# Turning q in 64x64 tiles, nine tokens a partition, next to the scores of the preceding pair

## The chip, the cores and the metric

The kernel runs on one core of one Trainium2 chip. The metric is device time in microseconds, the median of several executions. Shorter is better.

A core has five engines that run at the same time and meet at semaphores. TensorE (PE) multiplies matrices and turns (transposes) tiles, and writes to PSUM. VectorE (DVE) and ScalarE (ACT) read PSUM and compute on elements. GpSimd (POOL) computes on elements in SBUF. SyncE (SP) issues most of the DMA transfers here. Each engine takes its instructions strictly in the order in which the program gives them, and an instruction that waits holds up those behind it on its engine. For SP that makes a queue: a transfer can't be issued before the ones ahead of it have been.

## The reference

Eight batches of eight heads with 576 tokens of 64 numbers go through an attention of two parts, and the sum goes through a layer with an ELU between two matrix products. Cut to its core:

```python
q_d, k_d, v_d = means of 4 neighbouring tokens           # 144 coarse tokens
out_up = repeat(softmax(q_d k_d^T / 8) v_d, 4)           # far part
mask = abs(pos[:, None] - pos[None, :]) < 4
out_local = softmax(where(mask, q k^T / 8, -1e9)) v      # near part
x = (out_up + out_local) as [4608 tokens, 8 heads * 64 = 512]
h = x @ w_in                                             # 512 -> 2048
out = where(h > 0, h, exp(min(h, 0)) - 1) @ w_out        # 2048 -> 512
```

All arrays come in and go out as float32. On PE the kernel computes in float16.

## The kernel before

**Pairs.** Two heads are handled together and make a pair; a batch has four (j = 0 to 3). Heads e = 0 and 1 of a pair stand on partitions 0 to 63 and 64 to 127, with the 64 numbers of a head along the partitions and the tokens along the free dimension. To get q into this form it must be turned. For batches 2 to 7 this goes in five steps:

1. `load_qk` (line 206) loads q and k of a pair as float32 through SP. q comes as 96 partitions with six tokens of each of the two heads, k from batch 3 on as 96 partitions with twelve rows of 64.
2. `cast_qk` (line 232) has POOL cast both to float16. q's cast also brings the two heads of a token next to each other (line 242). Behind each cast a copy of one element (`apart`, line 230) marks its end.
3. `transposes` (line 314) turns q on PE: six transposes of 96 partitions x 128 columns (line 329) into the PSUM tile `tqk`. For batches 0 and 1, cast by the DMA, the heads are turned one by one into the upper and the lower half (line 324). k is turned on PE up to batch 2; from batch 3 on `flip` (line 804) does it by a transposing DMA, issued on SP as soon as POOL has cast k.
4. `evict_q` (line 355) has ACT copy q to SBUF in the order of the tokens (line 359).
5. `sums` (line 374) forms the coarse tokens: for q on POOL in two adds (lines 395, 397), for k on DVE (line 378).

`pair_transposes` (line 813) calls steps 3 to 5.

**Scores and outputs.** `pair_scores` (line 901) computes the near scores, 20 matmuls on 64x64 tiles (line 459), and the coarse ones (line 472, 8 matmuls), ACT takes the exponential (line 482) and DVE multiplies by the mask (line 497). `denominators` sums for a whole batch (line 519), DVE takes the reciprocal `rc` (line 525). For batches 3 to 7 the reciprocals are spread over the partitions by way of DRAM: `spread_out` (line 531) writes `rc` to `rd`, and `spread_in` (line 540) reads it back, repeated, as `rcb`, in two transfers. Both are issued on SP. `pair_outputs` multiplies by v (lines 603, 623), in batches 3 to 6 for pairs 0 and 1 together and then for pairs 2 and 3; `normalise` has DVE multiply by `rcb` (lines 667, 672) and POOL add the near and the far part into `xt` (line 684).

**The layer.** The 4608 tokens are cut into nine blocks of 512. `mm1` (line 720, four matmuls a step, 16 steps a block) and `mm2` (line 740, four matmuls a step) are interleaved, mm2 one block behind. Between them ACT takes the exponential (line 724) and DVE finishes the ELU (lines 725, 726). The attention of the next batches runs in between these steps.

**PSUM.** The tiles `tqk`, `sc`, `vs` and `lg` of two banks come from one turn of buffers (`two`, line 134), two of them once the first stage is over. A tile can be written when the earlier tile in its buffer has been read.

**The order** is written out by hand. Each action is an event with a time, and the program is issued in the order of these times; they aren't microseconds but slots, one step of mm1 and one of mm2 each, 16 to a block. For batches 4 to 7 the times stand in `LATER` (4 to 6) and `LAST` (7), counted from the first step of mm1 of the block with the batch's number; `tr` is `pair_transposes`, `sc` `pair_scores`, `cast` the casts, `dn` the denominators, `so` `spread_out`, `si` `spread_in`, `out` `pair_outputs`. Since a block is 16 slots long, the time t of batch b stands at t + 16 in the count of batch b - 1. Around a cast stand, from line 983 on:

```python
            at(p["cast"][j], cast_v, b, j)
            if b > 1:
                at(p["cast"][j] - 0.1, cast_qk, b, j)
                at(p["cast"][j] + 0.1, load, n + 3)
            if b >= FLIP:
                at(p["cast"][j] + 0.02, flip, b, j)
            at(p["tr"][j], pair_transposes, b, j)
            at(p["sc"][j], pair_scores, b, j)
```

`load` (line 968) issues q, k and v (four transfers) of the pair three further on, whose buffers the cast has just read. So the place of a cast also sets where one transposing DMA and six loads stand in SP's queue. The stores of the results (line 748) stand in the same queue.

Of the kernel before, what the change touches and what calls it, by code (L numbers as in the profile page):

```python
# [16 lines left out]
SD = S // 4  # L17
# [21 lines left out]
def _np_consts():  # L39

    f16 = np.float16
    off = np.arange(KW) - PAD
    m = np.zeros((KW, NB, QB), dtype=f16)
    for c in range(NB):
        for u in range(QB):
            ok = (np.abs(off - u) < 4) & (off + QB * c >= 0) & (off + QB * c < S)
            m[ok, c, u] = 1.0
    m = m.reshape(KW, S)
    neg = ((m - 1) * 30000).astype(f16)
    rs = np.zeros((QB, 3, SD), dtype=f16)  # L50
# [10 lines left out]
    return np.eye(KW, dtype=f16), neg, rs.reshape(QB, 3 * SD), vr, ind  # L61


def _np_windows():
# [39 lines left out]
def kernel(  # L104
# [101 lines left out]
    def load_qk(b, j, held=False):  # L206

        got = []
        for src, name in ((q, "q"), (k, "k")):
            a = src[b, 2 * j]  # L210
            t = sb.tile([QB, 2 * NB, D], FP32, tag=name + "32", bufs=3, name=name + "32")
            if held:
                nc.vector.memset(t[0:1, 0, 0:1], 0.0)
            runs_ = name == "q" or b < FLIP
            nc.sync.dma_start(
                out=t[:].rearrange("p (e r) d -> p e (r d)", e=2) if runs_ else t[:],
                in_=bass.AP(
                    tensor=a.tensor, offset=a.offset,
                    ap=[[TPP * D, QB], [S * D, 2], [1, TPP * D]] if runs_
                    else [[D, QB], [QB * D, 2 * NB], [1, D]],  # L220
                ),
            )
            got.append(t)
        qk32[(b, j)] = got
# [7 lines left out]
    def cast_qk(b, j, half=False):  # L232

        got = []
        for t, name in list(zip(qk32.pop((b, j)), ("q16", "k16")))[:: 1 if b < FLIP else -1]:
            x = sb.tile([QB, NB, 2, D], FP16, tag=name, bufs=4, name=name)
            src = t[:].rearrange("p (e c) d -> p c e d", e=2)
            if half:
                act(out=x[:, :, 0, :], in_=src[:, :, 0, :])
                dve(out=x[:, :, 1, :], in_=src[:, :, 1, :])  # L240
            else:
                nc.gpsimd.tensor_copy(out=x[:], in_=src)  # L242
                apart(x[0:1, 0, 0, 0:1])
            got.append(x)
# [69 lines left out]
    def transposes(b, j, fill=(0, 0)):  # L314
# [3 lines left out]
        for x, t, name, n in zip(xs, tr_tiles(b), ("tq", "tk"), fill):  # L318
            s[name] = t
            keep(t, n)  # L320
            for c in range(NB):
                if is_cast(b, j):
                    for e in range(2):
# [31 lines left out]
    def evict_q(b, j, copy):  # L355
        s = st[(b, j)]
        qt = s["q"] = QT[j]
        to, got = in_order(s["tq"], qt[:, 0:S])
        copy(out=to, in_=got)  # L359
        s["qt"] = [qt[:, QB * c : QB * c + QB] for c in range(NB)]  # L360

# [56 lines left out]
    def masked_scores(j, g, sc):  # L418
# [2 lines left out]
        r = [slice(64 * e, 64 * e + 64) for e in range(2)]  # L421
        for e in range(2):
            nc.tensor.matmul(
                sc[0:KW, 512 * e : 512 * e + HB], C["ID"][:],
                C["NEG"][:, HB * g : HB * g + HB], start=True, stop=False,
            )
        for n in range(3):
# [327 lines left out]
    def keep(t, n):  # L755

        for _ in range(n):
            if t.dtype == FP32:
                nc.tensor.matmul(t[:, 0:512], Z[:, 0:128], Z[:, 0:512], start=True, stop=True)  # L759
            else:  # L760
                for _ in range(4):
                    nc.tensor.transpose(t[0:KW, 0:KW], Z[0:KW, 0:KW], C["ID"][:])

    def first():
        nc.vector.memset(Z[:], 0.0)
# [46 lines left out]

    def pair_transposes(b, j):
        transposes(b, j)
        evict_q(b, j, act)
        if b < FLIP:
            evict_k(b, j, act)
# [3 lines left out]
    def selections(name):  # L821

        if name == "SEL":
            t = C[name] = sb.tile([KW, 1280], FP16, tag=name, bufs=1, name=name)
            src, parts = C["ID"], ((0, 5, 0), (5, 5, 64))
            step = 32
        else:
            src = sb.tile([KW, 16], FP16, tag="I4", bufs=1, name="I4")
            nc.vector.tensor_reduce(
                out=src[:], in_=_free(C["ID"][:, 0:1], [[1, 16], [32, NPAIR]]), axis=AX.X, op=AB.add  # L830
            )
            t = C[name] = sb.tile([KW, 1024], FP16, tag=name, bufs=1, name=name)
            parts, step = ((0, 8, 0),), 8
# [64 lines left out]
    def at(time, fn, *args):  # L898
        events.append((time, len(events), fn, args))

    def pair_scores(b, j):
        sc = two("sc")
        scores(j, sc)
        coarse(b, j, sc)
        exps(b, j, sc, 0, WL)
        exps(b, j, sc, WL, SD + SH)
        mask(b, j)
# [67 lines left out]
        2: dict(tr=[8.521, 19.14, 20.81, 24.84], sc=[16.66, 21.68, 23.15, 26.21], cast=[6.002, 15.82, 19.12, 20.36], dn=[28.71], vs=[29.1], sp=[30.02, 30.15, 29.43, 32.38], out=[30.72, 32.86, 33, 33.03], so=[17.79], si=[28.4]),  # L975
        3: dict(tr=[25.32, 29.24, 30.74, 34.58], sc=[28.69, 32, 36.48, 37.89], cast=[21.15, 25.5, 25.89, 28.85], dn=[40.9], vs=[40.84], so=[41.77], si=[43.95], out=[46.72, 47.24, 48.76, 48.78]),
    }
    LATER = dict(tr=[-27.78, -24.81, -17.34, -16.19], sc=[-25.74, -22.03, -14.56, -12.79], cast=[-32.93, -27.69, -22.54, -19.07], dn=[-10.25], vs=[-10.47], so=[-9.791], si=[-6.96], out=[-4.288, -4.511, -3.148, -3.906])
    LAST = dict(tr=[-27.36, -24.54, -17.71, -14.25], sc=[-25.67, -22.06, -15.67, -11.26], cast=[-32.18, -27.83, -24.84, -20.85], dn=[-9.492], vs=[-9.098], so=[-9.367], si=[-5.664], out=[-2.829, -4.665, -4.912, -2.635])
    for b in range(4, B):  # L980
        z = mm1_at(b, 0)
        PLAN[b] = {k: [z + x for x in a] for k, a in (LATER if b < B - 1 else LAST).items()}
    for b in range(1, B):
        p = PLAN[b]
        for j in range(NPAIR):
# [61 lines left out]
```

## Time and profile before

| | before |
|---|---|
| median of 3 runs | 351.66 us (351.36 to 353.28) |
| span of the profiled execution | 355.1 us |
| PE busy | 336.1 us, 95% of the span |
| DVE, ACT, POOL busy | 236.4, 180.3, 160.8 us |
| mean granted clock of PE | 0.976 |
| casts of q on POOL (line 242) | 24, 828 ns each |
| transposes of q on 96 partitions (line 329) | 144 |
| packets of all DMA transfers | 100304, 48.89 MB |

The profiled execution has its span as its only time; it is 1% above the median of the runs that were timed without a profile. In the rows that are shown, L and a number is the line of the kernel, `out<-in` names what is written and read, and x with a number is a count. A row of the timeline gives start and length in microseconds; matmuls overlap, so the time that a group takes is read from its start to the start of the next one. In brackets stands how long the engine was idle before, and what ended that. SPq is SP's queue: its rows are the issuing of a transfer, not the transfer.

### The profile page before, as it was taken

Reading aid. Unit: us, or ns where it says so; the run is one execution under the profiler, and the core shown is the slowest. Engines: PE = TensorE matmul, PEld = TensorE weight load, DVE = VectorE, ACT = ScalarE, POOL = GpSimd, SP = SyncE. Lnnn points to the kernel's source line nnn. Section 1 sums busy time; section 2 is a strip of 40 time slices with the busy share of each in tenths; the row PEclk is TensorE's granted clock in tenths of the full one; section 3 lists DMA queues with packets and bytes.
Section 4 is the critical chain, followed back from the end, with each engine's and each line's share of the span. In section 5 each row is a group of like instructions: output and inputs, shape, how many; then the busy total and the mean of one; then the engine's idle time right before and its main releaser. Section 6 shows DMA issues by size and latency. Waiting matters only on the chain.

```text
span 355.1 us, 10487 instructions
## 1 busy us (share of the span) xinstructions
PE 336.1 (95%) x4288; PEld 185.5 (52%) x4288; DVE 236.4 (67%) x466; ACT 180.3 (51%) x312; POOL 160.8 (45%) x298
## 2 busy tenths in 40 slices
PE   7993998799979999999999999999999999999996
PEld 3762885344545454545454555555455544444443
DVE  2334799566789877987697789768755855555510
ACT  4580587225755664466456645663553444444421
POOL 4464449279495834974397449855300500000000
PEclk9998799959999999999999999999999999999999
DMA  8999979997999698998979796943004010011012
GB/s 173 184 166 203 191 172 216 215 186 185 189 152 224 120 205 168 167 185 174 181 155 206 158 218 144 188 123 61 30 32 118 31 59 30 31 46 43 31 59 89
DMA packets 100304, 48.89 MB, mean 138 GB/s; under 512 B 81617, under 2 KB 95265, under 8 KB 100257
## 3 DMA queue, kind: packets, MB, share of 16 engines
q1 hardware_dynamic: 94417, 41.86, 57.8%
q0 software_dynamic: 5600, 6.26, 10.8%
q8 instruction: 33, 0.54, 0.7%
q10 hardware_dynamic: 240, 0.11, 0.2%
q14 instruction: 14, 0.11, 0.1%
HBM read 41.97 MB, written 9.55 MB: 145 GB/s over the span
## 4 chain that ended last, share of the span: by engine, by line
PE 72%; DMA 13%; DVE 6%; ACT 3%; issue 2%; POOL 2%; SPq 1%; DVEq 0%; POOLq 0%; ACTq 0%
PE op L740 31%; PE hp L720 28%; DMA v<-in_v_dram 6%; DMA rcb<-rd 3%; DMA WO<-in_moe_w_out_dram 3%; DVE ln L672 2%; PE sc L759 2%; PE tqk L329 2%; DMA rd<-rc 2%; PE lg L603 2%; DVE e L725 1%; PE sc L459 1%; ACT e L724 1%; DVE gt L726 1%; PE lg L623 1%
## 5 line engine op out<-in xcount | busy, mean ns | idle before, releaser
L740 PE MATMUL op<-WO,gt 128*128 128x512 f16 (+2 forms) x592 | 147.0, 377 | 1.0 <-DVE gt L726 0.6
L724 ACT ACTIVATE e<-hp 128x512 f16<-128x512 f32 x144 | 86.1, 599 | 110.5 <-PE hp L720 95.7
L720 PE MATMUL hp<-xt,WI 128*128 128x512 f16 x512 | 133.4, 384 | 0.7 <-DVE gt L726 0.5
L726 DVE SCALAR_TENSOR_TENSOR gt<-hp,e 128x512 f16<-128x512 f32 x144 | 99.6, 692 | 6.4
L725 DVE TENSOR_SCALAR e<-e 128x512 f16<-128x512 f16 x144 | 60.7, 421 | 58.1 <-ACT e L724 57.6
L740 PEld LDWEIGHTS <-gt 128*128 128x128 f16 x592 | 55.6, 98 | 62.8 <-issue 3.0
L720 PEld LDWEIGHTS <-WI 128*128 128x128 f16 x512 | 55.5, 115 | 49.6 <-issue 3.1
L684 POOL TENSOR_TENSOR xt<-ln 128x128 f16<-128x128 f16 (+7 forms) x55 | 36.7, 695 | 50.8 <-DVE ln L672 50.8
L482 ACT ACTIVATE pex<-sc 128x580 f16<-128x580 f32 (+1 forms) x56 | 30.2, 596 | 9.7 <-PE sc L472 9.7
L395 POOL TENSOR_TENSOR t<-qt 128x288 f32<-128x288 f16 x27 | 18.1, 671 | 36.8 <-ACT qt L359 36.8
L303 POOL CAST v<-v 128x640 f16<-128x640 f32 (+1 forms) x32 | 24.2, 756 | 21.1 <-DMA v<-in_v_dram 21.0
L746 ACT COPY os<-op 128x512 f32<-128x512 f32 (+2 forms) x37 | 21.4, 577 | 19.3 <-PE op L740 19.1
L378 DVE TENSOR_REDUCE ke<-kt 128x145 f16<-128x580 f16 x28 | 21.0, 751 | 2.4 <-ACT kt L366 2.4
L359 ACT COPY qt<-tqk 128x576 f16<-128x576 f16 x28 | 17.9, 638 | 8.5 <-PE tqk L329 6.7
L699 PE MATMUL hp<-xt,WI 128*128 128x256 f16 x128 | 17.3, 288 | 4.6 <-issue 4.6
L672 DVE TENSOR_TENSOR ln<-lg,rcb 128x580 f16<-128x580 f32 x28 | 21.1, 752 | 0.0
L242 POOL CAST q<-q 96x768 f16<-96x768 f32 x24 | 19.9, 828 | 0.0
L242 POOL CAST k<-k 96x768 f16<-96x768 f32 x24 | 19.8, 825 | 0.1
L699 PEld LDWEIGHTS <-WI 128*128 128x128 f16 x128 | 13.6, 118 | 5.8 <-issue 4.7
L497 DVE TENSOR_TENSOR pex<-pex,MASK 128x580 f16<-128x580 f16 x28 | 14.0, 500 | 3.8 <-ACT pex L482 3.6
L397 POOL TENSOR_TENSOR qd<-t 128x144 f16<-128x144 f32 x27 | 12.4, 461 | 2.1
L459 PEld LDWEIGHTS <-kt 64*64 64x64 f16 x560 | 7.0, 108 | 11.7 <-issue 8.8
(113 smaller groups left out, 271.6 us busy)
## 6 DMA issues: line engine op xcount, KB each, us to landing
out_dram<-os SPq DMA_DIRECT2D x35, 256.0 KB, 2.2
v<-in_v_dram SPq DMA_DIRECT2D x111, 80.0 KB, 4.6
q<-in_q_dram SPq DMA_DIRECT2D x25, 288.0 KB, 4.1
k<-in_k_dram SPq DMA_DIRECT2D x25, 288.0 KB, 5.1
rcb<-rd SPq DMA_DIRECT2D x10, 364.0 KB, 4.6
WI<-in_moe_w_in_dram POOLq DMA_DIRECT2D x4, 512.0 KB, 10.9
WO<-in_moe_w_out_dram POOLq DMA_DIRECT2D x4, 512.0 KB, 9.2
q<-in_q_dram POOLq DMA_DIRECT2D x7, 144.0 KB, 7.2
```

The costliest lines, as they stand in the source:

```text
L242: nc.gpsimd.tensor_copy(out=x[:], in_=src)
L303: nc.gpsimd.tensor_copy(out=v16[:], in_=v32[:].rearrange("p (e c) d -> p c e d", e=2))
L482: nc.scalar.activation(out=s["p"][:, :, a : a + n], in_=g2(sc, a, n), func=AF.Exp, scale=SCALE / 16 if a else SCALE,)
L672: nc.vector.tensor_tensor(out=ln[:, 0 : 2 * WL].rearrange("p (m h u) -> p m h u", h=2, u=WQ), in0=_free(lg[:, 0:1], [[WQ, WM], [512, 2], [ ...
L684: eng.tensor_tensor(out=xt(t)[:, j, t0 - TBLK * t : t1 - TBLK * t], in0=ln[:, a:z], in1=_rep4(ln[:, ga : ga + (z - a) // 4]), op=AB.add,)
L699: nc.tensor.matmul(FS[i][:, 256 * f : 256 * f + 256], w_in(dc, 2 * n + f), xts[0][:, dc, 256 * h : 256 * h + 256], start=(f == dc == 0), s ...
L720: nc.tensor.matmul(hp, w_in(dc, fc), xts[t][:, dc, :], start=(dc == 0), stop=(dc == DMC - 1),)
L724: nc.scalar.activation(out=e, in_=hp, func=AF.Exp)
L725: nc.vector.tensor_scalar(out=e, in0=e, scalar1=1.0, scalar2=-1.0, op0=AB.min, op1=AB.add)
L726: nc.vector.scalar_tensor_tensor(out=to, in0=hp, scalar=0.0, op0=AB.max, in1=e, op1=AB.add)
L740: nc.tensor.matmul(op_[:, a:z], gts[t][:, fc, 128 * tt : 128 * tt + 128], WO[:, fc, a:z], start=(fc == 0), stop=(fc == FCN - 1),)
L746: nc.scalar.copy(out=os_[:, a:z], in_=op_[:, a:z])
```

## The change

q of batches 2 to 7 is loaded in another form. The two heads of a pair have 2 x 576 = 1152 tokens, 128 x 9. Partition p gets the nine tokens from 9p on, 2304 bytes in one run, so head 0 lies on partitions 0 to 63 and head 1 on 64 to 127. The cast on POOL is then 128 partitions x 576 elements in order. q is turned by 18 transposes of 64x64, nine for each head, on the tiles at (0, 0) and (64, 64) in turn; the identity grows from 112 to 128 rows for that. ACT's copy puts the tokens in order with nine instead of six columns apart.

From pair (4, 1) to (7, 3) the turning has no event of its own. It is done in `pair_scores` of the preceding pair: the 18 transposes stand right ahead of the scores, and ACT's copy, POOL's adds and DVE's sum over k between the coarse scores and the exponential. Pairs of batches 2 and 3 and pair (4, 0) keep their events. For batches 4 to 7 some casts get earlier times; `tr` stays in the tables but is no longer used beyond (4, 0).

```diff
@@ load_qk
             a = src[b, 2 * j]
+            if name == "q" and b > 1:
+                t = sb.tile([128, 9, D], FP32, tag="q32", bufs=3, name="q32")
+                if held:
+                    nc.vector.memset(t[0:1, 0, 0:1], 0.0)
+                nc.sync.dma_start(
+                    out=t[:], in_=bass.AP(
+                        tensor=a.tensor, offset=a.offset, ap=[[9 * D, 128], [D, 9], [1, D]]
+                    ),
+                )
+                got.append(t)
+                continue
@@ cast_qk
+            if name == "q16" and b > 1:
+                x = sb.tile([128, 9, D], FP16, tag="q16", bufs=4, name="q16")
+                nc.gpsimd.tensor_copy(out=x[:], in_=t[:])
+                apart(x[0:1, 0, 0:1])
+                got.append(x)
+                continue
@@ transposes
+            if name == "tq" and b > 1:
+                for c in range(9):
+                    for e in range(2):
+                        r = slice(64 * e, 64 * e + 64)
+                        nc.tensor.transpose(t[r, 64 * c : 64 * c + 64], x[r, c, :], C["ID"][r, r])
+                continue
@@ evict_q
+        if b > 1:
+            to = qt[:, 0:S].rearrange("p (a r) -> p a r", r=9)
+            got = _free(s["tq"][:, 0:1], [[1, 64], [64, 9]])
         copy(out=to, in_=got)
@@
     def pair_transposes(b, j):
         transposes(b, j)
+        pair_turned(b, j)
+
+    def pair_turned(b, j):
         evict_q(b, j, act)
@@
+    def joined(b, j):
+
+        n = NPAIR * b + j + 1
+        return divmod(n, NPAIR) if NPAIR * 4 < n < NPAIR * B else None
+
     def pair_scores(b, j):
+        nxt = joined(b, j)
+        if nxt:
+            transposes(*nxt)
         sc = two("sc")
         scores(j, sc)
         coarse(b, j, sc)
+        if nxt:
+            pair_turned(*nxt)
         exps(b, j, sc, 0, WL)
@@
-    LATER = dict(tr=[-27.78, -24.81, -17.34, -16.19], sc=[-25.74, -22.03, -14.56, -12.79], cast=[-32.93, -27.69, -22.54, -19.07], dn=[-10.25], vs=[-10.47], so=[-9.791], si=[-6.96], out=[-4.288, -4.511, -3.148, -3.906])
-    LAST = dict(tr=[-27.36, -24.54, -17.71, -14.25], sc=[-25.67, -22.06, -15.67, -11.26], cast=[-32.18, -27.83, -24.84, -20.85], dn=[-9.492], vs=[-9.098], so=[-9.367], si=[-5.664], out=[-2.829, -4.665, -4.912, -2.635])
+    LATER = dict(tr=[-27.78, -24.81, -17.34, -16.19], sc=[-25.74, -22.03, -14.56, -12.79], cast=[-32.93, -28.69, -25.54, -20.07], dn=[-10.25], vs=[-10.47], so=[-9.791], si=[-6.96], out=[-4.288, -4.511, -3.148, -3.906])
+    LAST = dict(tr=[-27.36, -24.54, -17.71, -14.25], sc=[-25.67, -22.06, -15.67, -11.26], cast=[-32.18, -28.83, -25.84, -20.85], dn=[-9.492], vs=[-9.098], so=[-9.367], si=[-5.664], out=[-2.829, -4.665, -4.912, -2.635])
@@
-            at(p["tr"][j], pair_transposes, b, j)
+            if NPAIR * b + j <= NPAIR * 4:
+                at(p["tr"][j], pair_transposes, b, j)
```

The rest of the diff makes the identity 128x128 and cuts it back to 112 where it was used as such. Batch 3 has its own table, with `so` at 41.77 and `si` at 43.95; block 4 begins at 67.52 in that count.

More of the change, by code (lines that the diff above doesn't have):

```diff
@@ L60, in _np_consts @@
         ind[:, 127 + 32 * n : 126 + 32 * n + z] = 0.0
-    return np.eye(KW, dtype=f16), neg, rs.reshape(QB, 3 * SD), vr, ind
+    return np.eye(128, dtype=f16), neg, rs.reshape(QB, 3 * SD), vr, ind
 def _np_windows():
@@ L423, in masked_scores @@
             nc.tensor.matmul(
-                sc[0:KW, 512 * e : 512 * e + HB], C["ID"][:],
+                sc[0:KW, 512 * e : 512 * e + HB], C["ID"][0:KW, 0:KW],
                 C["NEG"][:, HB * g : HB * g + HB], start=True, stop=False,
@@ L761, in keep @@
                 for _ in range(4):
-                    nc.tensor.transpose(t[0:KW, 0:KW], Z[0:KW, 0:KW], C["ID"][:])
+                    nc.tensor.transpose(t[0:KW, 0:KW], Z[0:KW, 0:KW], C["ID"][0:KW, 0:KW])
     def first():
@@ L824, in selections @@
             t = C[name] = sb.tile([KW, 1280], FP16, tag=name, bufs=1, name=name)
-            src, parts = C["ID"], ((0, 5, 0), (5, 5, 64))
+            src, parts = C["ID"][0:KW], ((0, 5, 0), (5, 5, 64))
             step = 32
@@ L829, in selections @@
             nc.vector.tensor_reduce(
-                out=src[:], in_=_free(C["ID"][:, 0:1], [[1, 16], [32, NPAIR]]), axis=AX.X, op=AB.add
+                out=src[:], in_=_free(C["ID"][0:KW, 0:1], [[1, 16], [32, NPAIR]]), axis=AX.X, op=AB.add
             )
```

## The prediction

> **What bounds the kernel now.** I read the page's shares first, then the span cut into stretches, then one stretch instruction by instruction, and last the chain of waits with SP's queue beside it.
>
> ```profile
> span 355.1 us, 10487 instructions
> PE 336.1 (95%) x4288; PEld 185.5 (52%) x4288; DVE 236.4 (67%) x466; ACT 180.3 (51%) x312; POOL 160.8 (45%) x298
> ...
> 60.00:80.00 20.00, 17.08 (x302) 9.22 (x302) 12.37 (x23) 5.88 (x9) 10.84 (x20) 0.76 1.04 202
> 120.00:300.00 180.00, 179.07 (x2270) 92.41 (x2269) 137.27 (x254) 95.32 (x165) 87.84 (x165) 1.00 0.65 134
> ```
>
> In the rows of stretches the columns are length, busy PE, weight loads, DVE, ACT and POOL, then granted clock, DMA share and GB/s. From 120 to 300 us PE is idle for about 1 us in 180: a cost on PE there is a cost in time, and nothing can be gained there except by taking PE work away. From 60 to 80 us it is idle for 2.9 us and the granted clock is 0.76; costs can hide there. But a full PE does not mean that nothing else is close. The chain of waits (start, length, what) goes through two transfers in batch 3 and again in batch 4:
>
> ```profile
> 134.31 5.59 DMA rcb<-rd
> ...
> 147.44 1.02 PE hp L720 x4
> ...
> 169.23 5.53 DMA rcb<-rd
> ```
>
> The reciprocals of a batch go to DRAM (rd) and come back repeated (rcb); DVE's normalising (L667, L672) waits for rcb, and it frees the PSUM that the outputs of pairs 2 and 3 need:
>
> ```profile
> 174.88 0.31 DVE L667 TENSOR_TENSOR ln<-lg,rcb 128x144 f16<-128x144 f32 x1 [0.90 <-DMA rcb<-rd]
> ...
> 176.80 0.35 PE L603 MATMUL lg<-pex,v 64*64 64x58 f16 x20 [0.49 <-DVE ln L672]
> ...
> 208.65 0.31 DVE L667 TENSOR_TENSOR ln<-lg,rcb 128x144 f16<-128x144 f32 x1
> ```
>
> In batch 4 DVE waits 0.90 us for rcb and PE then 0.49 us for DVE: rcb has no slack there. In batch 3 the chain runs the same way and ends in a PE matmul at 147.44. In batch 5 (208.65) there was no wait.
>
> **Part one: 18 small transposes for 6 large.** PE's timeline, start and length:
>
> ```profile
> 215.93 1.03 PE L740 MATMUL op<-WO,gt 128*128 128x512 f16 x4
> 216.79 0.42 PE L329 MATMUL tqk<-ID,q 96*128 96x96 f16 x6
> 217.05 1.03 PE L720 MATMUL hp<-xt,WI 128*128 128x512 f16 x4
> ...
> 218.78 1.03 PE L720 MATMUL hp<-xt,WI 128*128 128x512 f16 x4
> 219.73 0.35 PE L459 MATMUL sc<-qt,kt 64*64 64x58 f16 x20
> 219.92 0.27 PE L472 MATMUL sc<-qd,ke 64*64 64x144 f16 x8
> ```
>
> Lengths overlap, so costs are read from start to start. Four L740 take 0.86 us (215.93 to 216.79), six transposes 0.26 (43 ns each). Ahead of the 64x64 scores the same four take 0.95 (218.78 to 219.73): 0.09 to enter the small tiles. Twenty 64x64 score matmuls take 0.19, some 9 ns each on four tiles. The new transposes use two tiles, (0,0) and (64,64), in turn. The nearest row is the transposing of batch 1 on two column tiles:
>
> ```profile
> 45.93 0.45 PE L324 MATMUL tqk<-ID,q 96*64 96x96 f16 x12
> 46.21 0.42 PE L324 MATMUL tqk<-ID,k 96*64 96x96 f16 x12
> ```
>
> Twelve take 0.28 us, 23 ns each at 96 columns. With 64 columns and some overhead I take 18 ns, 0.33 us for 18. The bounds: 18 x 9 = 0.17 (the pace of four tiles) and 18 x 43 = 0.78 (no overlap at all).
>
> The Trainium skill, "TensorE: Matmul & The Clock Gate", sections "LDWEIGHTS (loading the stationary operand)" and "Weight-path perf modes", speaks against the change: a weight load costs its columns over 1.2 GHz and only one of 128 columns is loaded fast, so an estimate by that page is 18 x 53 ns = 0.96 us a pair, and 24 x 0.70 = 17 us in all instead of 2 (383 us). The score row disagrees (9 ns for a 64-column load and its matmul together), so the trace decides.
>
> Fifteen pairs, (4,1) to (7,3), stand next to scores and pay no tile change of their own: 15 x (0.33 - 0.26) = +1.0 us. Nine, batches 2 and 3 and (4,0), stand alone: each also pays the 0.09, 9 x 0.16 = +1.4, of which I count +1.0, since some of batch 2's lie beside idle PE. Together +2 us; by the bounds 15 x -0.09 + 9 x 0 = -1.4 and 15 x 0.52 + 9 x 0.61 = +13.3.
>
> **Part two: casting and loading q.** POOL's cast goes from 768 strided elements to 576 straight ones on 128 partitions:
>
> ```profile
> L303 POOL CAST v<-v 128x640 f16<-128x640 f32 x28 | 20.8, 744 | 12.3 <-DMA v<-in_v_dram 12.3
> L242 POOL CAST q<-q 96x768 f16<-96x768 f32 x24 | 19.9, 828 | 0.0
> ```
>
> At v's pace of 744 ns for 640 elements it takes 0.67 us, so 0.16 less, 24 times: 3.8 us of POOL, which is busy for 45% of the span and waits for others. I count nothing. The load keeps its bytes in fewer, longer runs; nothing again. ACT's copy keeps its 576 elements a partition.
>
> **Part three: what moves with the casts.** This decides. From batch 4 on the cast of pair 2 stands 3 slots earlier, in batches 4 to 6 at -25.54 instead of -22.54. With it go its flip of k (0.02 behind the cast) and, 0.1 behind it, the load of q, k and v three pairs on, all on SP. In the preceding batch's count (16 slots a batch) that is -9.54, where it was -6.54. spread_out (rd) stands at -9.791 and spread_in (rcb) at -6.96. So one flip and six load transfers, which stood behind rcb, now stand between rd and rcb in SP's queue, in batches 3, 4 and 5. For batch 3 (41.77 and 43.95) the cast goes from 44.98 to 41.98: the same. In batch 6 (next cast -25.84) they fall ahead of rd, and few loads are left. SP's queue in batch 4, before:
>
> ```profile
> 165.80 0.55 SPq L531 DMA_DIRECT2D rd<-rc  x1
> ...
> 168.59 1.25 SPq L540 DMA_DIRECT2D rcb<-rd  x2
> 169.94 1.24 SPq L808 DMA_TRANSPOSE kt<-k  x1
> 171.28 0.52 SPq L215 DMA_DIRECT2D q<-in_q_dram  x1
> ...
> 172.39 3.93 SPq L280 DMA_DIRECT2D v<-in_v_dram  x4
> 176.42 0.55 SPq L748 DMA_DIRECT2D out_dram<-os  x1
> ...
> 189.09 2.61 SPq L280 DMA_DIRECT2D v<-in_v_dram  x4
> ```
>
> From the flip (DMA_TRANSPOSE) over q, k and four v to the end of the store is 7.0 us (169.94 to 176.97). The four v also go out in 2.61 instead of 3.93, which makes 5.7. The flip itself waits for POOL to cast k, and POOL does that after the halving of the joined pair's q. From a transposing to that cast's end:
>
> ```profile
> 162.34 0.35 PE L459 MATMUL sc<-qt,kt 64*64 64x58 f16 x20
> ...
> 164.47 0.42 PE L329 MATMUL tqk<-ID,q 96*128 96x96 f16 x6
> ...
> 167.87 0.18 POOL L230 COPY apart<-k 1x1 f16<-1x1 f16 x1
> ```
>
> That is 3.58 us. The transposing now stands at the scores (162.34), so the flip can go at 165.9, about when rd has gone out (166.35). rcb then goes out at 166.4 + 5.7 to 7.0 = 172.1 to 173.4 instead of 168.59: 3.5 to 4.8 us later. Batches 3 and 5:
>
> ```profile
> 128.32 0.35 PE L459 MATMUL sc<-qt,kt 64*64 64x58 f16 x20
> ...
> 133.67 1.25 SPq L540 DMA_DIRECT2D rcb<-rd  x2
> ...
> 197.04 0.35 PE L459 MATMUL sc<-qt,kt 64*64 64x58 f16 x20
> ...
> 202.00 1.60 SPq L540 DMA_DIRECT2D rcb<-rd  x2
> ...
> rcb<-rd SPq DMA_DIRECT2D x10, 364.0 KB, 4.6
> ```
>
> Flip at 128.32 + 3.58 = 131.9, so rcb at 137.6 to 138.9, 3.9 to 5.2 late. In batch 5 flip at 200.6, rcb 4.3 to 5.6 late. The last row's 4.6 us to landing, from the second of the two issues (about 203.0), ends at 207.6, 1 us ahead of 208.65: 3.3 to 4.6 count. Queued behind the late rcb on DVE is its own work for mm1 (L725, L726), and on PE everything behind the outputs of pairs 2 and 3. I take off 0.3 a batch for PE's own lateness: sum 9.8 to 13.7, taken +12. If the loads just ahead slow rcb's landing, it is more.
>
> Two smaller moves cost nothing by their cover. At the joined scores ACT's copy of the next pair's q, POOL's halving and DVE's sum over k stand ahead of the exps and the mask:
>
> ```profile
> L359 ACT COPY qt<-tqk 128x576 f16<-128x576 f16 x28 | 17.9, 638 | 8.5 <-PE tqk L329 6.7
> ```
>
> The exps are 0.64 us later. Their first readers in a hurry are the denominators, 2.5 slots behind pair 3's scores; a slot is (197.04 - 162.34) / 16 = 2.2 us, so 5 us cover it. With that gone it would be 0.6 a batch. And cast_v of pair 3 now stands ahead of POOL's last adds (L684) in batches 4 and 5:
>
> ```profile
> 180.57 2.65 POOL L684 TENSOR_TENSOR xt<-ln 128x256 f16<-128x256 f16 x4
> ...
> 183.28 1.03 PE L720 MATMUL hp<-xt,WI 128*128 128x512 f16 x4
> ```
>
> The third of the four adds ends at 182.56, and PE's fourth matmul reads it at 183.93, 1.4 us later. The cast puts 0.74 ahead (less 0.16), and the two transposings that leave this place bring PE 0.5 nearer. 0.3 us is left, so I count 0; with the cover gone it would be some 0.3 a batch.
>
> **Part four: the clock.** Stalls of 3 to 5 us on PE can cost twice (columns as above):
>
> ```profile
> 30.00:34.00 4.00, 0.00 (x0) 0.00 (x0) 1.48 (x2) 0.00 (x0) 2.45 (x5) 0.88 1.24 194
> 34.00:40.00 6.00, 5.72 (x68) 4.18 (x68) 2.54 (x4) 1.08 (x2) 3.39 (x6) 0.51 1.33 214
> ```
>
> Four idle us, and the 6 us of work after them ran at half the clock: 3 us lost at most. I count one such loss, 2.5, since only the longest of the three stalls is like it.
>
> Sum: 2 + 12 + 2.5 = +16.5 on a span of 355.1. The median of the runs, 351.66, is 1% below that span, and the differences carry over: 368.
>
> **The rivals.**
> - The clock falls after all three stalls, and each costs 2.5 to 4.5 us: 351.7 + 14 + 7.5 to 13.5 = 373 to 379. For it: 60 to 80 us shows 0.76 with 2.9 idle us in all. Against: each stall has full work for 30 us on either side. The Trainium skill, "TensorE: Matmul & The Clock Gate", section "Why this matters for your kernels", has the rule for this: no idle gap of PE over some 3 us, or the clock is halved; the row at 30 us agrees.
> - rcb's delay is absorbed: the flips and loads go out faster than 5.7 us, or DVE's wait replaces waits that PE has anyway. Then only part one is left, 351.7 + 2 = 353.7 (351 to 355). Against: the chain has no slack in batches 3 and 4.
> - It gets faster. Four tiles' pace holds for two (0.17 us a pair, -1.4 in all), and casts and loads of q that end sooner take away up to half of the 2.9 idle us from 60 to 80: 351.7 - 1.4 - 1.4 = 349. It decides only if rcb is less than 1 us late, which needs SP to issue seven transfers in the time it now spends waiting for rd.
> - The two tiles don't overlap at all: 0.78 us a pair, +11 on the forecast, 379. The L324 row speaks against it.
>
> **How the numbers follow.** Forecast (none or one fall of the clock) 0.53, with its own range 361 to 373; three falls 0.20; absorbed 0.14; faster 0.08; no overlap 0.05. Range 355 to 378. What a measurement can tell is about 0.5%, as the three runs differ by that. Faster 0.07; within 0.5%: half of the absorbed case and a rest, 0.08; slower 0.85. Predicted 368.
>
> **What would show it.** In the changed profile: rd followed by DMA_TRANSPOSE, q, k, v in SP's queue, and rcb 6 to 8 us after rd (now 2.8 to 3.1); DVE's L667 waiting 3 to 5 us for rcb in batches 3, 4 and 5 and not in 6 and 7; PE idle as long before the second output group; the clock row after it. Transposes: 18 from start to start in 0.3 us. I am wrong if rcb goes out within 4 us of rd, or if PE has no idle time at those outputs.

## The result, and the profile after

The changed kernel takes 375.3 us (median of 4 runs, 374.5 to 375.9) against 352.5 (351.4 to 353.6) for the kernel before: 1.063 times [1.057, 1.068], or +22.8 us. The profiled execution spans 373.4 us. Forecast: 368, range 355 to 378. The direction and the place were right. But the time lies in the first rival, in which the clock falls after all three stalls (373 to 379, given 0.20), and not in the case that was forecast (one fall or none, 361 to 373, given 0.53). All ratios, here and below, are of the runs within 1.5% of the fastest of their kernel.

In the changed file the lines have moved: normalising is L693 and L698 (L667, L672 before), the second group of outputs L629 and L649 (L603, L623), mm1 L746 with L750 to L752 behind it (L720, L724 to L726), the flip L834 (L808), rd and rcb L557 and L566 (L531, L540), the denominators L545 (L519). The small transposes are L342.

SP's queue in batch 4 of the changed kernel (start, length, what):

```profile
167.84 1.13 SPq L557 DMA_DIRECT2D rd<-rc  x1
169.85 1.24 SPq L834 DMA_TRANSPOSE kt<-k  x1
171.18 0.53 SPq L215 DMA_DIRECT2D q<-in_q_dram  x1
171.76 0.42 SPq L226 DMA_DIRECT2D k<-in_k_dram  x1
172.28 2.62 SPq L297 DMA_DIRECT2D v<-in_v_dram  x4
174.99 0.55 SPq L774 DMA_DIRECT2D out_dram<-os  x1
175.59 2.03 SPq L566 DMA_DIRECT2D rcb<-rd  x2
```

One flip and six loads stand between rd and rcb, and rcb goes out 7.8 us after rd (2.8 before). DVE and PE some us later, with the idle time before an instruction in brackets:

```profile
183.08 0.31 DVE L693 TENSOR_TENSOR ln<-lg,rcb 128x144 f16<-128x144 f32 x1 [4.80 <-DMA rcb<-rd]
184.11 0.48 PE L629 MATMUL lg<-pex,v 64*64 64x58 f16 x20 [4.04 <-DVE ln L698]
185.00 0.47 PE L629 MATMUL lg<-pex,v 64*64 64x58 f16 x20 [0.34 <-DVE ln L698]
185.85 1.90 PE L746 MATMUL hp<-xt,WI 128*128 128x512 f16 x4
187.54 1.91 PE L766 MATMUL op<-WO,gt 128*128 128x512 f16 x4
```

Where before PE waited 0.49 us it now waits 4.04 and 0.34, and the four L746 behind take 1.69 us from start to start (185.85 to 187.54) instead of 0.86. That is half the clock. The waits of the whole execution (us in total, times, longest), then stretches (length; busy PE, weight loads, DVE, ACT, POOL; granted clock, DMA share, GB/s):

```profile
DVE ln L693 <- DMA rcb<-rd: 14.7, 3, 5.2
PE lg L629 <- DVE ln L698: 12.9, 7, 4.5
```

```profile
120.00:300.00 180.00, 165.78 (x2336) 84.60 (x2336) 122.51 (x228) 83.93 (x146) 81.81 (x158) 0.94 0.57 126
120.00:160.00 40.00, 35.82 (x524) 18.14 (x524) 26.09 (x49) 17.48 (x31) 18.23 (x36) 0.91 0.75 160
160.00:200.00 40.00, 35.10 (x463) 17.51 (x462) 25.73 (x48) 18.05 (x32) 20.71 (x40) 0.91 0.69 149
200.00:240.00 40.00, 35.18 (x510) 17.94 (x508) 25.87 (x49) 18.16 (x32) 20.89 (x42) 0.91 0.66 142
...
180.09:183.50 3.41, 0.00 (x0) 0.00 (x0) 0.42 (x2) 0.00 (x0) 0.00 (x0) 1.00 0.66 170
183.50:186.91 3.41, 2.46 (x59) 1.55 (x60) 3.38 (x7) 0.00 (x0) 2.77 (x5) 0.50 0.02 5
186.91:190.32 3.41, 3.41 (x9) 1.18 (x8) 2.18 (x5) 0.60 (x1) 3.22 (x8) 0.50 0.32 50
```

Three waits for rcb, and with each comes a stretch like that from 183.50 to 190.32 us, 6.8 us at a granted clock of 0.50 (the other two begin at 142.54 and 224.46). In the three PE worked for 16.6 us at half the clock, which is 8.3 us of full-speed time lost. The measure used below is PE's time between the first denominator matmuls of successive batches: from batch 2 to batch 5 (the three stretches that hold the late rcb) it is 102.5 us before (126.72 to 229.20) and 123.7 after (123.57 to 247.22), +21.2. The two profiled spans differ by 18.3: outside the three stretches the profile after is 2.9 us shorter (that of the kernel before lies 1% above its runs).

### The profile page after: what moved, and what is told of

The parts are those of the page before. It is cut to its first block, busy times and chain, and to the rows that moved or that the text cites. A ratio compares the mean times of both kernels' runs of the same rounds, so it can differ in the third digit from the quotient of the medians.

```text
span 373.4 us, 11059 instructions
## 1 busy us (share of the span) xinstructions
PE 345.0 (92%) x4576; PEld 188.2 (50%) x4576; DVE 234.4 (63%) x466; ACT 179.8 (48%) x312; POOL 157.8 (42%) x298
## 4 chain that ended last, share of the span: by engine, by line
PE 75%; DVE 8%; DMA 7%; ACT 3%; issue 3%; POOL 1%; SPq 1%; DVEq 0%; POOLq 0%; ACTq 0%
PE op L766 30%; PE hp L746 28%; DMA rcb<-rd 5%; DMA WO<-in_moe_w_out_dram 3%; PE tqk L342 2%; DVE ln L698 2%; PE sc L785 2%; DVE e L751 2%; DVE gt L752 2%; PE hp L725 2%; PE lg L629 1%; ACT e L750 1%; PE sc L485 1%; PE lg L649 1%; SPq L566 1%
## 5 line engine op out<-in xcount | busy, mean ns | idle before, releaser
L750 ACT ACTIVATE e<-hp 128x512 f16<-128x512 f32 x144 | 86.2, 600 | 129.0 <-PE hp L746 118.1
L746 PE MATMUL hp<-xt,WI 128*128 128x512 f16 x512 | 137.4, 393 | 2.3 <-DVE gt L752 2.3
L752 DVE SCALAR_TENSOR_TENSOR gt<-hp,e 128x512 f16<-128x512 f32 x144 | 99.6, 692 | 6.4
L751 DVE TENSOR_SCALAR e<-e 128x512 f16<-128x512 f16 x144 | 57.9, 402 | 69.4 <-ACT e L750 69.0
L766 PEld LDWEIGHTS <-gt 128*128 128x128 f16 x592 | 56.4, 99 | 65.7 <-issue 5.4
L746 PEld LDWEIGHTS <-WI 128*128 128x128 f16 x512 | 56.2, 116 | 55.9 <-issue 7.2
L710 POOL TENSOR_TENSOR xt<-ln 128x128 f16<-128x128 f16 (+7 forms) x55 | 36.5, 691 | 58.8 <-DVE ln L698 58.8
L421 POOL TENSOR_TENSOR t<-qt 128x288 f32<-128x288 f16 x27 | 18.3, 676 | 51.8 <-ACT qt L385 51.8
L385 ACT COPY qt<-tqk 128x576 f16<-128x576 f16 x28 | 17.8, 637 | 11.9 <-PE tqk L342 7.2
L404 DVE TENSOR_REDUCE ke<-kt 128x145 f16<-128x580 f16 x28 | 21.0, 749 | 3.1 <-ACT kt L392 3.1
L629 PE MATMUL lg<-pex,v 64*64 64x58 f16 x560 | 9.9, 204 | 13.9 <-DVE ln L698 12.9
L259 POOL CAST k<-k 96x768 f16<-96x768 f32 x24 | 21.1, 878 | 0.0
L698 DVE TENSOR_TENSOR ln<-lg,rcb 128x580 f16<-128x580 f32 x28 | 21.1, 752 | 0.0
L693 DVE TENSOR_TENSOR ln<-lg,rcb 128x144 f16<-128x144 f32 x28 | 8.4, 300 | 16.2 <-DMA rcb<-rd 14.7
L629 PEld LDWEIGHTS <-v 64*64 64x64 f16 x560 | 7.5, 118 | 20.0 <-DVE ln L698 15.3
L249 POOL CAST q<-q 128x576 f16<-128x576 f32 x24 | 15.8, 659 | 0.0
```

The costliest lines, as they stand in the source:

```text
L629: nc.tensor.matmul(lg[64 * e : 64 * e + 64, 512 * h + to : 512 * h + to + n], w, st[(b, j)]["p"][64 * h : 64 * h + 64, e, a : a + n], star ...
L698: nc.vector.tensor_tensor(out=ln[:, 0 : 2 * WL].rearrange("p (m h u) -> p m h u", h=2, u=WQ), in0=_free(lg[:, 0:1], [[WQ, WM], [512, 2], [ ...
L710: eng.tensor_tensor(out=xt(t)[:, j, t0 - TBLK * t : t1 - TBLK * t], in0=ln[:, a:z], in1=_rep4(ln[:, ga : ga + (z - a) // 4]), op=AB.add,)
L746: nc.tensor.matmul(hp, w_in(dc, fc), xts[t][:, dc, :], start=(dc == 0), stop=(dc == DMC - 1),)
L750: nc.scalar.activation(out=e, in_=hp, func=AF.Exp)
L751: nc.vector.tensor_scalar(out=e, in0=e, scalar1=1.0, scalar2=-1.0, op0=AB.min, op1=AB.add)
```

## The experiments

The kernel before took 353.4 us (350.5 to 354.7) beside the first four kernels; the other eight were run on other chips. Each ratio is to the kernel before on the same chip. The stretches are of the profiled execution, batch 2's denominators to batch 5's. The last column splits their sum into PE's idle time, the time lost to the slow clock (half of what PE worked at 0.50), and the rest, PE's work at full speed.

| kernel | ratio [95%] | the three stretches, us | idle + slow clock + work |
|---|---|---|---|
| before | 1 | 34.0, 34.7, 33.8 | 0.9 + 0 + 101.6 |
| changed | 1.063 [1.057, 1.068] | 41.2, 41.7, 40.8 | 13.9 + 8.3 + 101.5 |
| casts_alone | 1.047 [1.039, 1.054] | 41.6, 38.5, 40.8 | 12.0 + 7.6 + 101.3 |
| casts_loads_behind | 1.000 [0.993, 1.006] | 34.7, 34.6, 33.8 | 1.4 + 0 + 101.7 |
| loads_behind | 1.020 [1.012, 1.028] | 37.0, 34.4, 34.8 | 3.8 + 0 + 102.4 |
| rcb_first | 1.051 [1.043, 1.059] | 40.2, 38.6, 40.3 | 11.6 + 6.3 + 101.3 |
| filled | 1.058 [1.052, 1.065] | 43.0, 39.0, 41.6 | 7.6 + 3.4 + 112.6 |
| join_old_casts | 1.046 [1.037, 1.055] | 40.1, 38.8, 39.6 | 11.0 + 5.9 + 101.6 |
| turn_alone | 1.001 [0.997, 1.006] | 36.4, 34.6, 34.7 | 1.6 + 0 + 104.2 |
| loads_behind_cast3 | 1.013 [1.004, 1.022] | 39.6, 34.2, 35.8 | 5.3 + 1.7 + 102.5 |
| loads_behind_apart | 1.021 [1.015, 1.027] | 36.5, 35.0, 36.0 | 5.0 + 0 + 102.5 |
| turn_alone_apart | 1.011 [1.004, 1.018] | 34.6, 36.5, 34.7 | 1.6 + 0 + 104.2 |
| joined_only_apart | 1.003 [0.998, 1.009] | 37.4, 34.6, 37.0 | 6.0 + 0 + 103.0 |
| before_apart | 1.002 [0.997, 1.007] | 38.2, 34.8, 35.0 | 5.4 + 0 + 102.5 |

**Only the new times of the casts, on the kernel before (casts_alone).**

```diff
-LATER = dict(... cast=[-32.93, -27.69, -22.54, -19.07] ...)
+LATER = dict(... cast=[-32.93, -28.69, -25.54, -20.07] ...)
-LAST = dict(... cast=[-32.18, -27.83, -24.84, -20.85] ...)
+LAST = dict(... cast=[-32.18, -28.83, -25.84, -20.85] ...)
```

> The kernel before, with nothing but the new cast times (pair 2 three slots earlier, pairs 1 and 3 one slot): q is still turned in six transposes by its own events. Theory (the flip and the six loads between rd and rcb on SP, and the clock after the stalls): almost the whole loss comes back, 368 to 375 us, rcb 6 to 8 us after rd in batches 3 to 5 and DVE's L667 waiting 3 to 5 us for it. Rival (the 64x64 turning, or its place at the scores, costs the time, and the wait for rcb only shows it): 351 to 354 us.

368.99 us (367.2 to 370.6). Its SP queue and its waits:

```profile
166.38 0.55 SPq L531 DMA_DIRECT2D rd<-rc  x1
167.04 1.86 SPq L808 DMA_TRANSPOSE kt<-k  x1
...
173.43 1.26 SPq L540 DMA_DIRECT2D rcb<-rd  x2
```

```profile
DVE ln L667 <- DMA rcb<-rd: 14.0, 3, 6.2
PE lg L603 <- DVE ln L672: 11.8, 7, 3.9
```

Without a single new transpose, the moved casts cost some 16 of the 23 us, by the late rcb.

**The same, with only pair 2's load held back behind rcb (casts_loads_behind).**

```diff
-                at(p["cast"][j] + 0.1, load, n + 3)
+                at(p["cast"][j] + (2.64 if j == 2 and 3 < b < 7 else 0.1), load, n + 3)
```

> The kernel before with two things changed: the new times of the casts, and the load of pair 2 in batches 4 to 6 held back until after spread_in, where it stood. The turning is the old one. Theory (in the run of the new casts alone, +16 us, the late rcb was all): 351 to 355 beside 353.4, rcb 3 to 4 us after rd. Rival (what is left over in the changed kernel with loads held back, +7 us, comes from the moved casts: the values of pair 3 are cast ahead of POOL's last adds and a DVE operation beside them takes 2.8 us): 356 to 360, with an L725 of 2.8 us on DVE and a 2.5-us wait of PE for it.

No difference to the kernel before: 1.000. The moved flip stays between rd and rcb and costs nothing; the six loads are the whole price. The pair of runs isolates it: 4.7% of the time, and 120.9 against 103.1 us in the three stretches, 17.8 us. PE idles 10.6 us longer in casts_alone, whose waits at the second outputs come to 11.4 (3.72 + 0.50, 2.43 + 0.50, 3.89 + 0.34), and loses 7.6 to the slow clock (0.91, 0.96 and 0.91 in the mean of 40 us), where casts_loads_behind loses nothing; its work hardly differs.

**The changed kernel with that load held back (loads_behind).** The same edit, on the changed kernel.

> The changed kernel with one edit: the loads that go with the cast of pair 2 (batches 4 to 6) are issued 2.64 slots behind the cast instead of 0.1, so they stand behind rcb on SP again; the flip stays between rd and rcb, where SP waits for rd to land anyway. Theory: rcb goes out about 3 us after rd as before, no stall, no fall of the clock: 352 to 355 us (what is left is the turning, 0.27 us from start to start at the scores against 0.26, and 0.2 us more at each of the nine that stand alone). Rival (turning and place): still above 365 us. Rival (the joined order alone delays DVE or POOL): something in between, 356 to 362 us.

359.6 us (358.1 to 360.5): missed by 5, and inside the rival of 356 to 362 in which DVE or POOL is delayed. rcb goes out 2.9 to 4.0 us after rd, and the waits for it come to 1.8 us:

```profile
164.96 1.19 SPq L557 DMA_DIRECT2D rd<-rc  x1
166.96 1.24 SPq L834 DMA_TRANSPOSE kt<-k  x1
168.30 0.53 SPq L774 DMA_DIRECT2D out_dram<-os  x1
168.92 1.27 SPq L566 DMA_DIRECT2D rcb<-rd  x2
```

So 4.3 of the 6.3% go, but a wait of 2.50 us that was in neither kernel has come in batch 3. POOL, DVE and PE there:

```profile
145.06 2.59 POOL L710 TENSOR_TENSOR xt<-ln 128x320 f16<-128x320 f16 x4
147.61 0.82 POOL L259 CAST k<-k 96x768 f16<-96x768 f32 x1
148.49 0.18 POOL L241 COPY apart<-k 1x1 f16<-1x1 f16 x1
145.78 2.80 DVE L751 TENSOR_SCALAR e<-e 128x512 f16<-128x512 f16 x1
149.22 0.28 DVE L751 TENSOR_SCALAR e<-e 128x512 f16<-128x512 f16 x1
149.36 1.05 PE L746 MATMUL hp<-xt,WI 128*128 128x512 f16 x4 [2.50 <-DVE gt L752]
```

An L751 that takes 0.28 us took 2.80: it started beside POOL's second add and ended at 148.58, during the one-element copy that follows POOL's cast of k. That joining is not needed for this is shown by turn_alone below, where an L751 took 2.57 us.

**rcb itself earlier (rcb_first).**

```diff
-si=[-6.96]   (LATER)        si=[43.95]   (batch 3)
+si=[-9.7]                   si=[41.9]
```

> The changed kernel with rcb moved instead: spread_in at -9.7 (batch 3: 41.9), right behind rd, so the flip and the loads of pair 2 wait on SP until rd has landed. Theory: rcb 3 us after rd, no stall at the outputs; but the flip goes out as late as before the change, while DVE's sum over k, which needs it, now stands at the preceding scores some 9 us earlier, so DVE may wait up to 3 us a batch with the ELU behind it: 353 to 361 us, above loads_behind. Rival (turning and place): above 365 us.

370.7 us (367.9 to 372.6): missed by 10, and in the rival's range. But the wait is the one that the theory named, only larger than its 3 us a batch: rcb is on time (2.1 to 3.5 us after rd), but the flip now stands behind it in SP's queue (171.29, where the changed kernel had 169.85), and DVE's sum over k, which the joining has moved ahead to the preceding pair's scores, waits for it:

```profile
DVE ke L404 <- DMA kt<-k: 16.9, 6, 6.1
PE hp L746 <- DVE gt L752: 12.1, 8, 4.0
```

A stall of the same size at another place, and much the same fall of the clock (0.96, 0.96, 0.91).

**Fill for PE ahead of the late outputs (filled).** Sixteen 128x512 matmuls of no use ahead of the second group of outputs in batches 3 to 5.

```diff
+        if 2 < b < 6 and js[0] == 2:
+            keep(one("fill"), 16)
         lgs = [two("lg") for _ in js]
```

> The changed kernel with 16 matmuls of 128x512 on zeros put on PE right ahead of the outputs of pairs 2 and 3 in batches 3, 4 and 5, where PE stands still for 3 to 5 us: 3.5 us of work that nothing reads. It only tells what the clock costs. Theory: the stall stays (rcb is as late as before), the clock stays at 1.00, and of the 23 us of loss the part that comes from the half clock goes: 364 to 369 us. If the clock has no part in it: 375 us or more, since the filling needs a PSUM buffer of mm2 and can cost up to 1 us a batch itself.

373.6 us, not 364 to 369. In the three stretches some 11 us of work for the fill (3.7 a batch) took the place of 6.3 us of idle time and 4.9 of slow clock, and the sum is what it was, 123.7. The mean clock is 0.96, 1.00 and 0.96, and the longest wait for rcb is still there:

```profile
DVE ln L693 <- DMA rcb<-rd: 16.2, 3, 6.3
PE lg L629 <- DVE ln L698: 4.5, 5, 2.0
```

```profile
150.77 1.47 PE L746 MATMUL hp<-xt,WI 128*128 128x512 f16 x4 [2.50 <-DVE gt L752]
```

Only batch 4 is as the experiment meant it: the fill takes up the stall, the clock stays at 1.00, and the stretch is 2.7 us shorter than in the changed kernel (39.0 against 41.7), about what the slow clock had cost there (2.9). In batch 3 a wait of 2.50 us for DVE has come that the changed kernel did not have, in batch 5 PE still waits 2.05 us for DVE, and the clock falls after both.

**The two halves of the change alone: turning without joining, joining with the old casts (turn_alone, join_old_casts).** In the first, all pairs are turned at `tr`, with the old cast times; in the second, only the cast times are the old ones.

```diff
 turn_alone, on the changed kernel (with the old cast lists):
-        return divmod(n, NPAIR) if NPAIR * 4 < n < NPAIR * B else None
+        return None
-            if NPAIR * b + j <= NPAIR * 4:
-                at(p["tr"][j], pair_transposes, b, j)
+            at(p["tr"][j], pair_transposes, b, j)
```

> The changed kernel with q turned in 64x64 tiles in all 24 pairs, but with each pair's turning at its old place by itself, and with the old times of the casts; nothing is joined and nothing moves on SP. Theory (a turning by itself costs 0.40 us and 0.10 us to enter the tiles, read in the changed profile, against 0.26 before): 24 x 0.24 = 5.8 us, so 357 to 360 beside 353.4 for the kernel before. The prediction's own price (0.16 us each, less in batch 2) would give 356 to 357; no cost at all, 353. rcb goes out 2.8 to 3.1 us after rd as before, and no wait of the normalising for rcb is among the longest.

> The changed kernel with the joining, but with the old times of the casts. rcb goes out on time again (within 3.5 us of rd). Theory: the joining needs the earlier casts, since pair 2's cast now stands only half a slot (1.1 us) ahead of its turning and POOL needs two casts of 0.7 to 0.8 us: PE waits 1 to 2 us for POOL ahead of the joined scores of pair 1 in batches 4 to 7, and DVE for the flip: 356 to 364. Rival (POOL runs ahead, the earlier casts were never needed): 353 to 355, with the joined turnings at 0.27 us.

Turning alone: 1.001, below what its durations promise. In its profile the three stretches are 3.3 us longer (105.8): 0.7 of it is idle time, with an L751 of 2.57 us and a wait of 1.39 in batch 3, and 2.6 is PE's work, 0.21 us for each of the 12 turnings there. By that price 24 would cost 5.1 us, an estimate, where the interval of the ratio leaves room for 2.1 at most (that of turn_alone_apart, below, for 6.3); this is not explained. Joining with the old casts: 1.046, and dearer than expected. PE does not wait for POOL as I had thought. The joining has moved DVE's sum over k (L404, and L378 in the kernel before) from its own turning to the preceding pair's scores, and the flip comes too late for it. SP and DVE in batch 4, and the waits:

```profile
173.50 1.24 SPq L834 DMA_TRANSPOSE kt<-k  x1
...
180.44 0.76 DVE L404 TENSOR_REDUCE ke<-kt 128x145 f16<-128x580 f16 x1 [5.68 <-DMA kt<-k]
```

```profile
DVE ke L404 <- DMA kt<-k: 14.0, 3, 5.7
PE hp L746 <- DVE gt L752: 11.6, 8, 3.6
```

In the kernel before the flip stood at the same place behind rcb (169.94), but the sum over k came only at 182.69, and nothing waited; here DVE stands still from 174.75 to 180.44 with the work for mm1 behind it. So the joining does need the earlier casts, and these take the loads ahead of rcb, unless the load is taken off the cast.

**What is left with rcb on time (loads_behind_cast3, and pauses on POOL in batch 3).** The first puts pair 3's cast back:

```diff
-LATER = dict(... cast=[..., -25.54, -20.07] ...)
+LATER = dict(... cast=[..., -25.54, -19.07] ...)
```

> The changed kernel with the load of pair 2 in batches 4 to 6 held back until after spread_in, as before, and pair 3's cast of batches 4 to 6 back at its old time (-19.07 instead of -20.07), so that POOL's last adds stand ahead of the casts again. Theory (pair 3's casts beside the adds stretch the DVE operation to 2.8 us): no L751 over 1.1 us, the 2.5-us wait of PE at 149 us gone, and 354 to 357 instead of 359.6. Rival (the rest is the turning by itself and has nothing to do with pair 3's casts): 358 to 360.

1.013, and an L751 of 2.87 us with a wait of 2.50 is still there: the place of pair 3's cast is not its cause. The other four have a one-element copy behind each add of batch 3:

```diff
                 in1=_rep4(...), op=AB.add,
             )
+            if b == 3:
+                apart(xt(t)[0:1, j, t1 - TBLK * t - 1 : t1 - TBLK * t])
```

> The changed kernel with the load of pair 2 held back until after spread_in (batches 4 to 6), and on POOL a one-element copy of the result behind each of the adds of batch 3 (L710), so that POOL pauses between them. Theory (the DVE operation that took 2.8 us could not start while POOL's operations stood back to back, and ran as soon as POOL stopped): no L751 over 1.1 us, no 2.5-us wait of PE for L752, batch 3's stretch between denominators 34.5 instead of 37.0 us, and 355 to 357.5 beside 359.6 for the kernel with the loads held back alone (353.4 for the kernel before, there). Rival (it is something else in that stretch, or the 2.5 us come back as another wait): 358 to 361.

> The kernel with all 24 turnings in 64x64 tiles, each by itself at its old place, with the old casts, and pauses on POOL in batch 3. It tells what the turning costs without the long DVE operation: by the durations in the profiles 24 x 0.24 = 5.8 us at most, 24 x 0.16 = 3.8 by the prediction's own price; measured with the long operation it was 1.0013 times the kernel before. Theory (the long operation cost 1.4 to 2.4 us of it): batch 3's stretch 34.5 instead of 36.4 us, and 0.995 to 1.003 times the kernel before; rival (nothing in it): as without the pauses.

> As the kernel with loads held back and pauses on POOL, but the 64x64 turning only for the fifteen pairs that stand next to scores, (4,1) to (7,3); the nine others are turned, cast and loaded as in the kernel before. Theory by the turnings read in the profiles (the nine alone cost 0.24 us each, the fifteen 0.01 each): 2 us less than that kernel, so 353 to 356. If the joining itself costs, by ACT's copy and POOL's halving ahead of the exps (0.6 us a batch), the two are equal within 1 us, and both stay 2 to 4 above the kernel before.

> The kernel before with the pauses on POOL in batch 3 alone, as a control. Its profile shows no L725 over 1.1 us, so the pauses should do nothing: within 0.5% of the kernel before. If it is faster by more, the pauses are worth something by themselves and the gains of the other three with them are not the long operation's.

With the pauses no L751 in batch 3 is long, in any of the kernels. But the time doesn't follow (1.021, where it was 1.020 without them; 1.011 for the turning alone, where it was 1.001). Other waits stand in the profiles instead. In loads_behind_apart PE waits 0.97 us for the last add in batch 3, and in batch 4, where there are no pauses, the long operation is back (its lines are two further down: L753 is L751):

```profile
179.55 2.60 POOL L710 TENSOR_TENSOR xt<-ln 128x256 f16<-128x256 f16 x4
182.11 0.82 POOL L259 CAST k<-k 96x768 f16<-96x768 f32 x1
182.99 0.18 POOL L241 COPY apart<-k 1x1 f16<-1x1 f16 x1
181.03 2.05 DVE L753 TENSOR_SCALAR e<-e 128x512 f16<-128x512 f16 x1 [0.80 <-ACT e L752]
183.85 1.02 PE L748 MATMUL hp<-xt,WI 128*128 128x512 f16 x4 [0.90 <-DVE gt L754]
```

The wait of mm1 for the last add comes with the pauses themselves. It stands in three of the four kernels that have them (0.97 to 1.38 us), and in none of the ten without. In the control:

```profile
147.81 0.38 PE L722 MATMUL hp<-xt,WI 128*128 128x512 f16 x1 [1.37 <-POOL xt L684]
```

So the pauses take away one delay and bring another. With the old turning for the nine single pairs the ratio is 1.003, and the runs of the control don't differ from the kernel before (1.002). Its one profile has 5.4 us of idle time in the three stretches all the same, where the kernel before has 0.9: one profile is too little to settle waits of 1 to 3 us. Against my expectation the nine seem to cost 1.8% beside joined turnings, yet all 24 alone cost 0.1 to 1.1%: the parts don't add up. The comparison is weak, since the twelve runs of joined_only_apart go from 352.8 to 366.7 us, with a median of 358.0, 1.0% above the kernel before. What is settled: no version that was run beats the kernel before, and joined turning with rcb on time lies 0 to 2% above it. Which of the small waits makes the 0 to 7 us is open.

## Why the prediction was right, point by point

- **Part three, the queue: right.** rcb was to go out 6 to 8 us after rd; it went out 7.5, 7.8 and 6.6 us after. DVE was to wait 3 to 5 us: 14.7 in three waits, the longest 5.2. PE's waits at the second outputs (2.54 + 0.40, 4.04 + 0.34, 4.48 + 0.34) sum to 12.1; +12 was taken. From the flip to rcb it was 5.7 us each time, the lower of the two figures for the queue. That this is caused by the six loads, and not by the flip or the casts, is shown by the two runs that differ in the load alone.
- **Part four, the clock: the term that was mis-sized.** "I count one such loss, 2.5, since only the longest of the three stalls is like it." With all three stalls the clock was 0.50 for 6.8 us, in which PE worked for 6.0, 5.9 and 4.7: 8.3 us lost where 2.5 were counted. The 21.2 us of growth in the three stretches are 13.0 of idle time and 8.3 of slow clock, while PE's work is the same (101.5 against 101.6). The reason that I gave against it, that full work stands for 30 us on either side, did not hold: the work around the three stalls was full, and the clock fell each time. The Trainium skill, "TensorE: Matmul & The Clock Gate", section "Why this matters for your kernels", asks for no gap over about 3 us; after the gaps of 4.04 and 4.48 us the traces agree, and they show the fall after shorter ones too (below).
- **Part one, the transposes: right in size.** Joined, 18 transposes with the scores and the coarse scores take 0.66 us (132.95 to 133.61, in the rows below) against 0.39 without them (before, 219.73 to the next L740 at 220.12): 0.27 for 18, 15 ns each, where 0.33 was taken and the six large ones took 0.26. Alone they take 0.40 (120.00 to 120.40). The estimate of 53 ns a load (17 us in all) is ruled out, and so is the rival without overlap. By PE's work in the three stretches a joined turning costs 0 to 0.07 us more than the old one (101.5 and 102.4 against 101.6, 12 turnings) and one alone 0.21. That is an estimate of 1.9 to 2.9 us for fifteen and nine, where 2 was counted; the runs themselves put all 24 alone at 0.1 to 1.1%, 0.4 to 3.9 us. The row at 132.95 below has 14 of the 18; the other four stand in two more rows, among the scores.

```profile
120.00 0.47 PE L342 MATMUL tqk<-ID,q 64*64 64x64 f16 x18
120.40 0.84 PE L746 MATMUL hp<-xt,WI 128*128 128x512 f16 x3
...
132.95 0.41 PE L342 MATMUL tqk<-ID,q 64*64 64x64 f16 x14
...
133.61 1.05 PE L746 MATMUL hp<-xt,WI 128*128 128x512 f16 x4
```

- **Part two, q's cast: right.** 659 ns against 828 (0.67 expected), and nothing of it is seen in the time.

```profile
L249 POOL CAST q<-q 128x576 f16<-128x576 f32 x24 | 15.8, 659 | 0.0
```

- **The smaller moves, counted at nothing: not shown either way.** ACT's copy ahead of the exps and the cast of v ahead of the adds are in loads_behind, which is 2% above the kernel before and not equal to it. Putting pair 3's cast back did not help; the copy was not tried alone.
- **The rivals.** Three falls: this is what happened. Absorbed, and faster: rcb was late in all three batches. No overlap: 15 ns a transpose and not 43. In numbers, 13.0 of idle time and 8.3 of slow clock make up the growth of the three stretches; the sum of 16.5 had the idle time about right (12) and lacked 5.8 of the clock, two of the three falls.

## What to carry to other kernels

An issue that is moved takes along everything scheduled relative to it: list what each queue holds between an issue and the wait that it must beat, and move only what the step needs (here the load could stay where it was, at no cost). A stall of PE long enough for its clock to fall is priced with the slow work behind it as well, once for each stall, however full the engine is otherwise (here 13.0 us of idle time cost 8.3 more). And where several things that others wait for share one queue, putting another first can just change the name of the wait, as in rcb_first.

## What the runs showed of the hardware that was not expected

**A stall of 2.5 us may or may not halve the clock, and its place in a step decides.** In every profile the granted clock is 1.00 or 0.50 and changes only at points that lie a multiple of 3.41 us apart, which stand elsewhere in each execution. Two kernels have the same wait of 2.50 us in batch 3, before 149.36 (loads_behind) and before 145.44 (loads_behind_cast3). Cut at these points, the steps around it are, in the first and in the second:

```profile
144.13:147.54 3.41, 2.73 (x13) 1.14 (x11) 3.38 (x5) 1.78 (x3) 3.35 (x7) 1.00 0.71 150
147.54:150.95 3.41, 1.59 (x8) 0.82 (x9) 2.62 (x4) 0.50 (x1) 2.75 (x7) 1.00 1.24 202
```

```profile
142.50:145.91 3.41, 0.91 (x6) 0.27 (x4) 3.34 (x4) 0.60 (x1) 3.28 (x7) 1.00 1.18 240
145.92:149.33 3.41, 3.41 (x10) 1.21 (x9) 1.38 (x3) 0.60 (x1) 0.58 (x2) 0.50 1.06 196
```

In the first the wait lies across two steps, PE is idle for 0.68 and 1.82 us of them, and the clock stays at 1.00. In the second it lies in one step, and the next is at 0.50. All 14 profiles agree from 105 to 330 us: each of the 15 falls follows a step in which PE was idle for 1.91 to 3.41 us, and no step at full clock with 1.82 or less was followed by one. A second step at 0.50 came where PE was idle for 0.87 us or more of the first (7 of the 15); where it was idle for 0.48 or less, the clock was back after 3.41 us. Before 105 us the clock also fell after steps with less idle time (0.98 us in the step from 67.45 of the changed kernel), so idle time is not the whole rule. The same stall of 2.50 us cost nothing beyond itself in the one kernel and 1.7 us of full-speed time in the other.

**A DVE operation held for ten times its length.** L751, 0.28 us otherwise, took 2.57 to 2.87 us beside POOL's adds in six kernels with the new turning, once in each, and 2.04 and 2.05 us in two more; in the kernel before none took over 1.09. In the rows shown above it ends (148.58, 183.08) during the one-element copy at which POOL pauses, not with the add that it met. In turn_alone, where no copy stands at that place, it ends at 147.17, just after POOL's second halving add has begun (147.09); that add, like the copy, needs the result of the instruction ahead of it. The Trainium skill, "SBUF — State Buffer", section "Who interferes with whom", says that a two-port DVE operation and a GpSimd instruction exclude each other for a whole instruction; the measured hold goes over several back-to-back POOL instructions. The pauses in batch 3 took it away there, which fits a shared port that POOL doesn't give up between instructions, but doesn't prove it.
